# The first layer's leaky activation: one ScalarE parametric ReLU in place of a ScalarE scaling and a VectorE maximum

## The chip, the cores and the metric

The kernel runs on one core of a Trainium2 chip. The metric is the device time of one execution in microseconds, the median over runs on the chip. TensorE is written PE, VectorE DVE, ScalarE ACT, GpSimd POOL and SyncE SP. Each engine executes its own instructions in the order in which they stand in its queue; engines wait for each other through semaphores.

## The reference

An attention with decaying states gives `x` (3072 tokens by 512), and two feed-forward layers follow it. Only the activation of the first layer is touched by the change.

```python
def _attn_ref(q, k, v):                       # B, H, S, D = 4, 8, 768, 64
    ...
    for t in range(S):
        state = gamma[None, :, None, None] * state + np.einsum('bhd,bhe->bhde', k[:, :, t], v[:, :, t])
        y[:, :, t] = scale * np.einsum('bhd,bhde->bhe', q[:, :, t], state)

def _moe_ref(x, w_in, w_out):                 # 512 -> 2048 -> 512
    h = x @ w_in
    g = np.maximum(0.01 * h, h)
    return (g @ w_out).astype(np.float32)

def _moe2_ref(x, w_in, w_out):                # 512 -> 2048 -> 512
    h = x @ w_in
    g = h * np.cos(h)
    return (g @ w_out).astype(np.float32)
```

## The kernel before, in words

**Products.** Every large product is made three times in `float32r`, of a high and a low part of each operand (`mm3`, L232 to L234: high by high, low of the weights by high, high by low of the data). The two feed-forward layers go over 6 blocks of 512 tokens (`n`) and 16 slices of 128 hidden columns (`f`), one iteration each. In an iteration PE makes the hidden product `hp` (`gemm1`, 12 matmuls of 128x512, into a PSUM bank) and adds an earlier iteration's activated slice to the four accumulators `acc` (`gemm2_a`, 12 matmuls).

**The activation.** It is made in two parts. `begin` stands in the iteration of the product, on ACT: `t = 0.01 * hp` (L450). `finish` stands in the next iteration, on DVE, and reads PSUM again: `t = max(hp, t)` (L457). Behind it `high_g` rounds `t` to `gh` on ACT (L481) and `low_g` takes `gl = t - gh` on DVE or POOL (L486). `hp` has two PSUM banks in the first layer, so the `gemm1` two iterations later can begin only when the last reader of its bank is done. In three of the first 32 iterations, chosen by a table `SPL`, `begin` is two ReLUs on ACT (L446, L448) and `finish` a subtraction on POOL (L455), and DVE has no part in it.

**The order around it.** The order of instructions is written out by hand and nothing is rescheduled. A product waits in `pending` until its second half is due, so that `gemm2_a` follows its `gemm1` by three iterations in the first segments. The first layer runs in segments (`SEGMENTS`): block 0 with its first 7 slices, block 1 with its first 4, block 0 with the other 9, block 1 with the other 12, then blocks 2 to 5 whole. In the first four segments the first layer's weights are still being prepared, because they arrive as float64 bits and are rounded on the chip: for each of 32 halves of a slice ACT makes an exponent and scales a word (L114, L116), DVE makes three bit operations (L119, L122, L127), POOL adds (L132), ACT writes the high part (L135) and POOL the low part (L138; twice it is DVE). These "ticks" (`Weights`, table `TICKS`) stand between the instructions of the iterations, as do steps of attention (`PLAN`) for the tokens to come: `scores` with its mask on DVE (L359), `pv` with its scalings on DVE (L398), its high part on ACT (L409) and its low part on POOL (L410). From block 2 on the second layer's weights are rounded in the same way and put aside in DRAM (`early_steps`).

**Queues.** SP issues nearly all transfers, in the order of the program. None of them is issued by an instruction that the change touches.

Of the kernel before, what the change touches and what calls it, by code (L numbers as in the profile page):

```python
# [17 lines left out]
AF = mybir.ActivationFunctionType  # L18
ALU = mybir.AluOpType
PSUM = bass.MemoryType.PSUM  # L20
DRAM = bass.MemoryType.DRAM
# [53 lines left out]
def body(ctx: ExitStack, tc: tile.TileContext, att, w1, w2, tab, out):  # L75
    nc = tc.nc
# [18 lines left out]
    def stage(tag="o"):  # L95
        return tmp.tile([P, BLK], F32, tag=tag, name=tag, bufs=4 if tag == "o" else 2)
# [3 lines left out]
    # Weights arrive as the bits of float64. A half of a slice is read into the place that its  # L100
    # two float32r parts take later: [high part | low part], 512 columns each.
# [10 lines left out]
    # The instructions that round pairs of words (low, high) to float32, in their order, and then split it.  # L112
    def exponent(raw, t):
        nc.scalar.activation(out=t.bitcast(F32), in_=raw[:, :, 1].bitcast(F32), func=AF.Abs)  # L114
        # The low word in units of float32's last place, to the nearest.
        nc.scalar.mul(out=raw[:, :, 0], in_=raw[:, :, 0].bitcast(U32), mul=2.0**-29)  # L116
# [25 lines left out]
    class Weights:  # L142
        """Rounds the halves in turn: in one tick the first part of one half and the second part of the half
        before, instruction by instruction in turn, and the start of the next half."""
# [44 lines left out]
        def step(self):  # L189
            """The next instruction or two of a tick."""  # L190
            if not self.run:
                self.run = self.pieces()
            next(self.run, None)

        def tick(self):
            """All that is left of the tick under way, or one more."""
            self.step()
            while self.run:
                self.step()

    # The second layer's (f, 1) halves are rounded ahead of their turn, one at a time, and wait in DRAM.
# [34 lines left out]
    # ------------------------------------------------------------ attention  # L236
    def make_attention(apool, ps_att, tb):
        # The states of two heads, block-diagonally too. They stand, as the values added to them,
        # enlarged by the decay since the start; the results are reduced by it.
        st = apool.tile([P, NPAIR, C], F32, name="st", bufs=1)  # L240
        # Queries of two heads stand block-diagonally, the other blocks zero.
# [7 lines left out]
        # Places that weights take later hold the first units' operands: [tile] and [tile][half].  # L249
# [114 lines left out]
        def cross(u):  # L364
            """What the chunks before give. A bank's products are one group: the first clears it."""
            c, half = (u // 2) % NCH, u % 2
            d = U[u]
            d["ps"] = ps = bank(u, "attB", 2)
            d["po"] = ps[:, : 2 * C].rearrange("p (a i) -> p a i", a=2)
            for a in range(2) if c > 0 else ():  # L370
                q = d["raw"][:, R_Q, a * C : a * C + C]
                nc.tensor.matmul(d["po"][:, a, :], st[:, 2 * half + a, :], q, start=a == 0, stop=False)

        def pv(u, xh, xl, tok0):
            """The unit's results, and the state behind it."""
# [43 lines left out]
    # ------------------------------------------------------------ one pass of a feed-forward layer  # L419
# [21 lines left out]
    # A layer's activation in two parts: `begin` for the product just computed, `finish` an iteration later.  # L441
    class Leaky:
        def begin(self, hp, split=False):
            t = stage("t")
            if split:
                nc.scalar.activation(out=t, in_=hp, func=AF.Relu)  # L446
                o = stage()
                nc.scalar.activation(out=o, in_=hp, func=AF.Relu, scale=-0.01)  # L448
                return hp, t, o
            nc.scalar.mul(out=t, in_=hp, mul=0.01)  # L450
            return hp, t

        def finish(self, hp, t, o=None):
            if o is not None:
                nc.gpsimd.tensor_tensor(out=t, in0=t, in1=o, op=ALU.subtract)  # L455
                return t
            nc.vector.tensor_tensor(out=t, in0=hp, in1=t, op=ALU.max)  # L457
            return t
# [31 lines left out]
    with tc.manual_schedule():  # L490
        # ======================================================== first feed-forward layer, attention ahead of it
        with ExitStack() as actx:
# [15 lines left out]
            # Steps of attention, with the next unit's preparation and scores under way: two for each  # L508
            # of the second block's units, five for each later pair.
# [37 lines left out]
            # The halves of the first layer's weights in the order of their first use.  # L547
# [25 lines left out]
            # The sine's table holds every other function here as well: it is loaded once, at the start.  # L573
# [99 lines left out]
            SPL = ('1001000', '0000', '000000001')  # L673
# [3 lines left out]
            for seg, (n, f0, f1) in enumerate(SEGMENTS):  # L677
# [18 lines left out]
                for f in range(f0, f1):  # L696
# [21 lines left out]
                    begun = leaky.begin(hp, seg < 3 and SPL[seg][f - f0] == '1')  # L718
# [11 lines left out]
        # ======================================================== second feed-forward layer  # L730
# [59 lines left out]
```

## Time and profile before

| | before |
|---|---|
| runs | 1186.72, 1188.00, 1188.61 us (median 1188.0) |
| profiled execution, first to last instruction | 1187.5 us |
| PE busy (matmul) | 1154.6 us, 97% |
| DVE busy | 702.5 us, 59% |
| ACT busy | 490.8 us, 41% |
| POOL busy | 448.1 us, 38% |

The profiled execution has no time of its own beside its span; its span lies 0.5 us below the median of the runs. Busy shares are means over the whole span, in which stages with different limits follow each other. A matmul's end is modelled, so that a busy PE is not a PE at its peak, and idle time of an engine is shown with the instruction of another engine that ended it.

### The profile page before, as it was taken

Reading aid. Unit: us, or ns where it says so; the run is one execution under the profiler, and the core shown is the slowest. Engines: PE = TensorE matmul, PEld = TensorE weight load, DVE = VectorE, ACT = ScalarE, POOL = GpSimd, SP = SyncE. Lnnn points to the kernel's source line nnn. Section 1 sums busy time; section 2 is a strip of 40 time slices with the busy share of each in tenths; the row PEclk is TensorE's granted clock in tenths of the full one; section 3 lists DMA queues with packets and bytes.
Section 4 is the critical chain, followed back from the end, with each engine's and each line's share of the span. In section 5 each row is a group of like instructions: output and inputs, shape, how many; then the busy total and the mean of one; then the engine's idle time right before and its main releaser. Section 6 shows DMA issues by size and latency. Waiting matters only on the chain.

```text
span 1187.5 us, 15236 instructions
## 1 busy us (share of the span) xinstructions
PE 1154.6 (97%) x5728; PEld 955.4 (80%) x5728; DVE 702.5 (59%) x997; ACT 490.8 (41%) x893; POOL 448.1 (38%) x398
## 2 busy tenths in 40 slices
PE   6988899999999999999999999999999999999998
PEld 5767778887888888888888888888888888888887
DVE  7899777655646545543466555555555655555553
ACT  4546553433444334432355443333433333333332
POOL 5676674342324333320156353233232332232222
PEclk9999999999999999999999999999999999999999
DMA  9905505234223223300465300200200200100000
GB/s 344 307 1 185 170 19 174 93 126 158 85 93 120 94 97 116 125 19 1 142 222 204 131 20 1 71 1 1 71 1 1 71 1 1 62 1 1 36 1 36
DMA packets 36361, 100.96 MB, mean 85 GB/s; under 512 B 4032, under 2 KB 6208, under 8 KB 36288
## 3 DMA queue, kind: packets, MB, share of 16 engines
q1 hardware_dynamic: 36144, 99.73, 24.5%
q8 instruction: 45, 0.74, 0.3%
q10 hardware_dynamic: 144, 0.26, 0.1%
q14 instruction: 28, 0.23, 0.1%
HBM read 76.91 MB, written 23.07 MB: 84 GB/s over the span
## 4 chain that ended last, share of the span: by engine, by line
PE 84%; DVE 8%; DMA 4%; issue 1%; ACT 1%; POOL 1%; SPq 0%; ACTq 0%; DVEq 0%; POOLq 0%
PE hp L232 13%; PE acc L232 13%; PE hp L234 13%; PE hp L233 13%; PE acc L233 13%; PE acc L234 13%; DMA w<-w 2%; DVE cbuf L119 2%; DVE cbuf L122 1%; DVE cbuf L127 1%; DMA cbuf<-w 1%; DVE gl L486 1%; DVE t L457 1%; PE attA L383 1%; PE attB L383 1%
## 5 line engine op out<-in xcount | busy, mean ns | idle before, releaser
L232 PE MATMUL hp<-xh,w 128*128 128x512 f32 x768 | 302.0, 393 | 16.2 <-DVE t L457 16.2
L234 PE MATMUL hp<-xl,w 128*128 128x512 f32 x768 | 300.5, 391 | 0.6 <-POOL xl L410 0.6
L233 PE MATMUL hp<-xh,w 128*128 128x512 f32 x768 | 300.0, 391 | 0.0
L486 POOL TENSOR_TENSOR gl<-r,gh 128x512 fp32r<-128x512 f32 x96 | 124.5, 1298 | 300.9 <-ACT gh L481 263.2
L468 DVE SCALAR_TENSOR_TENSOR r<-k,hp 128x512 f32<-128x512 int32 x96 | 66.0, 688 | 230.4 <-ACT k L467 226.9
L232 PEld LDWEIGHTS hp<-xh,w 128*128 128x128 f32 x768 | 144.6, 188 | 50.6 <-DVE t L457 19.3
L234 PEld LDWEIGHTS hp<-xl,w 128*128 128x128 f32 x768 | 144.8, 188 | 31.7 <-POOL xl L410 1.1
L233 PEld LDWEIGHTS hp<-xh,w 128*128 128x128 f32 x768 | 145.0, 189 | 29.3
L472 DVE SCALAR_TENSOR_TENSOR r<-k,r 128x512 f32<-128x512 int32 x96 | 151.6, 1579 | 3.3
L232 PE MATMUL acc<-gh,w 128*128 128x512 f32 x384 | 152.0, 396 | 0.1
L233 PE MATMUL acc<-gh,w 128*128 128x512 f32 x384 | 150.1, 391 | 0.2 <-POOL w L138 0.2
L234 PE MATMUL acc<-gl,w 128*128 128x512 f32 x384 | 149.6, 390 | 0.0
L473 ACT ACTIVATE r<-r,bias 128x512 f32<-128x512 f32 x96 | 69.5, 724 | 193.4 <-DVE r L472 193.4
L232 PE MATMUL acc<-w,gh 128*128 128x512 f32 x384 | 149.4, 389 | 0.0
L233 PE MATMUL acc<-w,gl 128*128 128x512 f32 x384 | 149.4, 389 | 0.0
L234 PE MATMUL acc<-w,gh 128*128 128x512 f32 x384 | 149.4, 389 | 0.0
L467 ACT ACTIVATE k<-hp,bias 128x512 int32<-128x512 f32 x96 | 66.2, 690 | 125.5 <-PE hp L234 125.4
L481 ACT CAST gh<-t 128x512 fp32r<-128x512 f32 x96 | 59.6, 621 | 138.2 <-DVE t L457 89.9
L138 POOL TENSOR_TENSOR w<-cbuf,w 128x512 fp32r<-128x512 f32 x46 | 63.4, 1377 | 72.9 <-ACT w L135 71.3
L132 POOL TENSOR_TENSOR cbuf<-cbuf,w 128x512 int32<-128x512 int32 x48 | 68.7, 1431 | 49.3 <-DVE cbuf L127 49.3
L232 PEld LDWEIGHTS acc<-gh,w 128*128 128x128 f32 x384 | 72.2, 188 | 15.9 <-issue 0.5
L234 PEld LDWEIGHTS acc<-gl,w 128*128 128x128 f32 x384 | 72.2, 188 | 15.3
(122 smaller groups left out, 1589.5 us busy)
## 6 DMA issues: line engine op xcount, KB each, us to landing
w<-w SPq DMA_DIRECT2D x48, 512.0 KB, 6.9
raw<-att SPq DMA_DIRECT2D x32, 512.0 KB, 4.4
cbuf<-w SPq DMA_DIRECT2D x16, 512.0 KB, 3.7
w2d<-cbuf SPq DMA_DIRECT2D x16, 512.0 KB, 2.9
w<-w2d SPq DMA_DIRECT2D x16, 512.0 KB, 3.2
w<-att SPq DMA_DIRECT2D x14, 512.0 KB, 7.4
x2d<-o SPq DMA_DIRECT2D x24, 256.0 KB, 3.1
o<-x2d SPq DMA_DIRECT2D x24, 256.0 KB, 4.2
```

The costliest lines, as they stand in the source:

```text
L119: nc.vector.tensor_scalar(out=t.bitcast(F32), in0=t.bitcast(F32), scalar1=MIN_HI, scalar2=None, op0=ALU.max)
L132: nc.gpsimd.tensor_tensor(out=t, in0=t, in1=raw[:, :, 0], op=ALU.add)
L138: eng.tensor_tensor(out=w[:, 512:1024], in0=t.bitcast(F32), in1=w[:, 0:512].bitcast(F32), op=ALU.subtract)
L232: nc.tensor.matmul(o, sh, mh, start=start, stop=False)
L233: nc.tensor.matmul(o, sl, mh, start=False, stop=False)
L234: nc.tensor.matmul(o, sh, ml, start=False, stop=stop)
L467: nc.scalar.activation(out=k, in_=hp, func=AF.Identity, bias=self.bias[:, 0:1], scale=INV_2PI)
L468: nc.vector.scalar_tensor_tensor(out=r, in0=k, scalar=-C1, in1=hp, op0=ALU.mult, op1=ALU.add)
L472: nc.vector.scalar_tensor_tensor(out=r, in0=k, scalar=-C2, in1=r, op0=ALU.mult, op1=ALU.add)
L473: nc.scalar.activation(out=r, in_=r, func=AF.Sin, bias=self.bias[:, 1:2], scale=1.0)
L481: nc.scalar.copy(out=gh, in_=g)
L486: eng.tensor_tensor(out=gl, in0=g, in1=gh.bitcast(F32), op=ALU.subtract)
```

## The change

`begin` becomes one ACT instruction, a parametric ReLU with slope 0.01 that reads `hp` from PSUM and writes `t`; `finish` gives `t` back and issues nothing. The split form and its table `SPL` go. Everything else stands where it stood: `high_g` and `low_g` follow an iteration later. (Comments were taken out as well, so that line numbers shift: the parametric ReLU is L445 in the changed file, `high_g` L472 and `low_g` L477.)

```diff
     class Leaky:
-        def begin(self, hp, split=False):
+        def begin(self, hp):
             t = stage("t")
-            if split:
-                nc.scalar.activation(out=t, in_=hp, func=AF.Relu)
-                o = stage()
-                nc.scalar.activation(out=o, in_=hp, func=AF.Relu, scale=-0.01)
-                return hp, t, o
-            nc.scalar.mul(out=t, in_=hp, mul=0.01)
-            return hp, t
-
-        def finish(self, hp, t, o=None):
-            if o is not None:
-                nc.gpsimd.tensor_tensor(out=t, in0=t, in1=o, op=ALU.subtract)
-                return t
-            nc.vector.tensor_tensor(out=t, in0=hp, in1=t, op=ALU.max)
+            nc.scalar.activation(out=t, in_=hp, func=AF.Prelu, alpha=0.01)
+            return (t,)
+
+        def finish(self, t):
             return t
...
-            SPL = ('1001000', '0000', '000000001')
...
-                    begun = leaky.begin(hp, seg < 3 and SPL[seg][f - f0] == '1')
+                    begun = leaky.begin(hp)
```

DVE's queue where block 0's first segment ends and block 1's begins (iterations of slices 5 and 6), before. `cbuf` holds a half in work, `w_1_647` is the raw half of the second part of slice 5, `st` and `w_0_115` belong to attention:

```order
104 L127 SCALAR_TENSOR_TENSOR cbuf<-w_1_647,cbuf 128x512
105 L457 TENSOR_TENSOR t<-hp,t 128x512
106 L398 SCALAR_TENSOR_TENSOR w_0_115<-attB,tb 128x128 x2
107 L407 TENSOR_TENSOR st<-st,attB 64x2x64 x2
108 L457 TENSOR_TENSOR t<-hp,t 128x512
109 L119 TENSOR_SCALAR cbuf<-cbuf 128x512
110 L122 TENSOR_SCALAR cbuf<-cbuf 128x512
111 L127 SCALAR_TENSOR_TENSOR cbuf<-w_1_699,cbuf 128x512
112 L486 TENSOR_TENSOR gl<-t,gh 128x512
```

The same place of DVE's queue in the changed kernel:

```order
101 L127 SCALAR_TENSOR_TENSOR cbuf<-w_1_642,cbuf 128x512
102 L398 SCALAR_TENSOR_TENSOR w_0_115<-attB,tb 128x128 x2
103 L407 TENSOR_TENSOR st<-st,attB 64x2x64 x2
104 L119 TENSOR_SCALAR cbuf<-cbuf 128x512
105 L122 TENSOR_SCALAR cbuf<-cbuf 128x512
106 L127 SCALAR_TENSOR_TENSOR cbuf<-w_1_692,cbuf 128x512
107 L477 TENSOR_TENSOR gl<-t,gh 128x512
```

The two maxima are gone, and what stood behind them follows at once; nothing else changes place.

ACT's queue at the same place, before (L409 is attention's high part, L135 a weight's):

```order
75 L135 CAST w_1_830<-cbuf 128x512
76 L450 ACTIVATE t<-hp 128x512
77 L114 ACTIVATE cbuf<-w_1_699 128x512
78 L116 ACTIVATE w_1_699<-w_1_699 128x512
79 L135 CAST w_1_857<-cbuf 128x512
80 L481 CAST gh<-t 128x512
81 L409 CAST xh<-w_0_115 128x2x128
82 L450 ACTIVATE t<-hp 128x512
83 L481 CAST gh<-t 128x512
```

And in the changed kernel:

```order
73 L135 CAST w_1_821<-cbuf 128x512
74 L445 ACTIVATE t<-hp 128x512
75 L114 ACTIVATE cbuf<-w_1_692 128x512
76 L116 ACTIVATE w_1_692<-w_1_692 128x512
77 L135 CAST w_1_848<-cbuf 128x512
78 L472 CAST gh<-t 128x512
79 L409 CAST xh<-w_0_115 128x2x128
80 L445 ACTIVATE t<-hp 128x512
81 L472 CAST gh<-t 128x512
```

The parametric ReLU stands exactly where the scaling stood, and is now the last reader of `hp`; `gh` follows in the same queue and no longer waits for another engine to finish `t`. Over the whole program DVE loses its 93 maxima, ACT three instructions and POOL three, PE and SP keep their order, and one load of ACT's function tables stands in the queue as before, at the start.

## Rows read from the trace of the kernel before

**Rows 1.** Stretches: us; busy PE, PEld, DVE, ACT, POOL (instructions); clock; DMA share, GB/s

```profile
43.00:172.00 129.00, 112.60 (x538) 89.05 (x538) 117.70 (x151) 75.69 (x145) 94.73 (x75) 0.97 0.36 122
...
107.70:111.10 3.40, 3.40 (x10) 2.61 (x9) 3.37 (x6) 3.40 (x7) 2.42 (x2) 0.50 0.36 128
162.30:165.70 3.40, 3.40 (x10) 2.62 (x9) 3.33 (x4) 2.35 (x5) 2.67 (x3) 0.50 0.00 0
...
200.00:656.00 456.00, 454.35 (x2453) 380.40 (x2451) 248.40 (x430) 179.93 (x357) 154.66 (x146) 1.00 0.34 117
656.00:1187.50 531.50, 527.61 (x2328) 436.71 (x2326) 289.01 (x312) 206.25 (x331) 160.85 (x124) 1.00 0.08 27
```

**Rows 2.** PE's waits: us in total, times, longest us

```profile
PE hp L232 <- DVE t L457: 16.2, 11, 2.9
...
PE attA L356 <- DVE sf L359: 2.1, 1, 2.1
```

**Rows 3.** PE's waits after 172 us alone

```profile
PE hp L232 <- DVE t L457: 2.4, 3, 0.9
```

**Rows 4.** Order of time on PE, DVE and ACT, two places: start, us

```profile
87.84 0.50 PE L232 MATMUL hp<-xh,w 128*128 128x512 f32 x1 [2.19 <-DVE t L457]
...
87.10 0.69 DVE L457 TENSOR_TENSOR t<-hp,t 128x512 f32<-128x512 f32 x1
...
80.91 0.61 ACT L450 ACTIVATE t<-hp 128x512 f32<-128x512 f32 x1
...
161.72 0.50 PE L232 MATMUL hp<-xh,w 128*128 128x512 f32 x1 [2.85 <-DVE t L457]
...
160.99 0.68 DVE L457 TENSOR_TENSOR t<-hp,t 128x512 f32<-128x512 f32 x1
...
157.62 0.59 ACT L450 ACTIVATE t<-hp 128x512 f32<-128x512 f32 x1
```

**Rows 5.** Groups by line: busy us, mean ns of one, idle before

```profile
L450 ACT ACTIVATE t<-hp 128x512 f32<-128x512 f32 x93 | 55.4, 596 | 26.1 <-PE hp L234 25.7
L446 ACT ACTIVATE t<-hp 128x512 f32<-128x512 f32 x3 | 1.8, 598 | 0.3 <-PE hp L234 0.3
L473 ACT ACTIVATE r<-r,bias 128x512 f32<-128x512 f32 x96 | 69.5, 724 | 193.4 <-DVE r L472 193.4
L574 ACT ACT_TABLE_LOAD x1 | 1.3, 1283 | 0.7 <-PEq L763 0.7
```

**Rows 6.** The same groups, of the stretch 43 to 172 us alone

```profile
L457 DVE TENSOR_TENSOR t<-hp,t 128x512 f32<-128x512 f32 x17 | 11.6, 684 | 2.1 <-ACT t L450 2.0
...
L455 POOL TENSOR_TENSOR t<-t,o 128x512 f32<-128x512 f32 x1 | 1.5, 1472 | 0.0
```

**Rows 7.** Waits of ACT and of POOL, 43 to 172 us

```profile
ACT gh L481 <- DVE t L457: 26.0, 15, 3.0
...
POOL w L138 <- ACT w L135: 22.3, 20, 2.0
```

**Rows 8.** Durations of two DVE lines, ns, least/median/most

```profile
L457 DVE TENSOR_TENSOR t<-hp,t x93: 674/684/694, 50.8 to 658.1; 128x512 f32<-128x512 f32 x93
...
L119 DVE TENSOR_SCALAR cbuf<-cbuf x64: 412/764/1537, 16.8 to 693.5; 128x512 f32<-128x512 f32 x64
```

**Rows 9.** Order of time, POOL and PE: parts made, then used

```profile
64.54 1.69 POOL L138 TENSOR_TENSOR w<-cbuf,w 128x512 fp32r<-128x512 f32 x1 [0.91 <-ACT w L135]
...
66.30 0.50 PE L232 MATMUL hp<-xh,w 128*128 128x512 f32 x1
...
152.44 1.47 POOL L486 TENSOR_TENSOR gl<-t,gh 128x512 fp32r<-128x512 f32 x1
...
156.43 0.39 PE L234 MATMUL acc<-gl,w 128*128 128x512 f32 x1
...
164.72 1.42 POOL L138 TENSOR_TENSOR w<-cbuf,w 128x512 fp32r<-128x512 f32 x1 [0.73 <-ACT w L135]
...
171.86 0.39 PE L233 MATMUL acc<-gh,w 128*128 128x512 f32 x1
```

## The prediction

> **What bounds the kernel now.** I read the stretches first. PE is busy for 454.35 of 456 us between 200 and 656 us and for 527.61 of 531.5 us after that, at full clock [rows 1]. Nothing that ACT or DVE does there can be on the path that sets the end. What is left lies early: from 43 to 172 us PE is busy for only 112.6 of 129 us, while DVE is busy for 117.7 us, 91% [rows 1]. That is where the first layer's weights are rounded beside the products.
>
> Then PE's waits. The largest by far is `hp` L232 waiting for the maximum L457: 16.2 us, 11 times [rows 2]; 2.4 us of it, three times, lie after 172 us [rows 3], so 13.8 us in eight waits lie in the early stretch. The next is a wait of attention for its mask, 2.1 us [rows 2].
>
> Then the order of time at such a wait shows why. At 87.84 us PE starts a `gemm1` after 2.19 us of idleness; its bank was released by a maximum that DVE began at 87.10 us, at once behind other work. The scaling of the same product, on ACT, had begun at 80.91 us and taken 0.61 us. At 161.72 us the same three steps stand at 161.72, 160.99 and 157.62 us [rows 4]. So ACT was done with `hp` 6.3 us and 3.5 us before PE needed the bank, and the bank was held only by DVE's queue, full of rounding.
>
> Last, the clock. In two stretches of 3.40 us, from 107.7 and from 162.3 us, the granted clock is 0.50, the lower level, 1.2 GHz [rows 1]. The second begins 0.6 us after the longest wait for L457, which ended at 161.72 us [rows 4].
>
> **The change, part by part.**
>
> *The price of the new instruction.* No parametric ReLU is in the trace. The scaling that it replaces takes 596 ns, a plain ReLU out of the same bank 598 ns; the dearest activation of this size, a sine with a bias operand, 724 ns [rows 5]. It has neither bias nor operand more than the ReLU, so I take 0.60 us, and 0.57 to 0.72 as bounds. The 96 instructions then cost ACT what the 93 scalings cost. At 0.72 us ACT would work 0.12 us more in an iteration of some 6 us: hidden, since ACT is busy for 75.7 of 129 us in the early stretch and 180 of 456 us in the middle [rows 1]. One table load of 1283 ns stands in the queue [rows 5], and the changed program has no second one.
>
> The Trainium skill ("ScalarE: Activation LUTs", Rules for kernel authors) says to make `relu` and `max` on VectorE and not on ScalarE, since VectorE can be up to three times as fast per element in bf16. By that rule the change would go the wrong way. The trace differs: in float32 the maximum takes 684 ns [rows 8] and comes on top of a scaling of 596 ns that ScalarE makes anyway [rows 5].
>
> *The release of the bank: -16.2 us.* `hp` now comes free where ACT's instruction ends, 3.5 to 6.3 us before PE asks for it in the two places shown; the others are like them. All 11 waits go [rows 2], as far as nothing else is late behind them. No new dependence comes in: `t`, `gh` and `gl` wait for what they waited for, less the maximum.
>
> *The clock: -3.4 us.* 3.40 us at half clock do 1.7 us of work; twice that is 3.4 us [rows 1]. If the clock does not fall, PE gains it. Bounds: 0 and 3.4. I take 3.4, because the stall before the second stretch is one of those removed, and I take the first to be alike.
>
> *What is late next: +4.4 us.* PE would then be 13.8 + 3.4 = 17.2 us earlier at 172 us than now, and what it eats must be ready earlier too. With rounding at its old times three places stop it [rows 9]. A low weight part is ready at 64.54 + 1.69 = 66.23 us and used by the second matmul from 66.30 us: almost no slack. A `gl` is ready at 153.91 and used at 156.43 us: 2.5 us. A low weight part is ready at 166.14 and used at 171.86 us: 5.7 us. Between the last two PE can still lose its wait of 2.85 us, so it could be 2.5 + 2.85 = 5.4 us earlier at 172 us.
>
> How much does rounding gain? From DVE 17 maxima leave, 11.6 us, and from POOL 1.5 us [rows 6]. But L119, which often follows a maximum, takes 412 to 1537 ns, while the maximum always takes 674 to 694 [rows 8]: L119 waits for POOL in that time, and where it does, an earlier start gains nothing. I count half, 5.8 us. ACT gains most. `gh` waits 26.0 us for the maximum in 15 waits, and all of ACT's queue waits with it, the high weight parts L135 too; POOL waits 22.3 us in 20 waits for L135 [rows 7], 1.12 us each, where 0.73 us is the bare way through ACT [rows 9]. So 20 x 0.39 = 7.7 us could go; as this overlaps with DVE's share I count half, 3.9 us. Sum: 5.8 + 1.5 + 3.9 = 11.2 us, and PE may be 5.4 + 11.2 = 16.6 us earlier at 172 us: 0.6 us short of 17.2. A tighter place is the bank itself. At 161.72 us PE would like to start 13.8 + 1.7 = 15.5 us earlier, at 146.2; ACT ends its instruction at 158.21 us now, and 11.2 us of gain less the 0.7 us or so that fall after it put that at 147.7: 1.5 us short. I add half of DVE's share, 2.9 us, which I trust least. That makes 4.4 us; bounds: 0, and 16.2 - 7.8 = 8.4 if rounding gains nothing (first rival).
>
> *Elsewhere: 0.* Between 200 and 1187.5 us PE is busy throughout, so there the maxima that leave DVE (nearly all of the other 76) and the ACT waits that go are hidden under PE; what PE has gained by 200 us it keeps to the end. The 2.1 us of attention [rows 2] I leave in: that mask stands behind `gl` and rounding on DVE, not behind a maximum.
>
> *Sum.* Against the profiled span: 1187.5 - 16.2 - 3.4 + 4.4 = 1172.3 us. The median of the runs is 0.5 us above the span: **1172.8 us**.
>
> **The rivals.**
>
> *Rounding keeps its pace.* DVE and POOL wait for each other: L119 takes up to 1537 ns, and a maximum that never varies may just fill time in which DVE's next instruction would have waited anyway. Then PE is 5.4 us earlier at 172 us, the three later waits give 2.4 us, the clock gives nothing since PE still waits, now for weights: 7.8 us, 1188.0 - 7.8 = 1180.2 us. For it speaks the spread of L119 [rows 8]; against it, that POOL waits for ACT and ACT for the maximum [rows 7], which has nothing to do with the order between DVE and POOL. The Trainium skill ("SBUF — State Buffer", Who interferes with whom) states the rule behind this rival: an instruction of VectorE with at most one SBUF input contends with GpSimd for nothing, one with two inputs or in a two-port mode does, and the later one is blocked for the whole instruction. By it the maximum, with one input from PSUM, frees nothing that rounding lacks. The trace agrees with it in the durations of the two lines [rows 8].
>
> *Everything goes.* Rounding always stays ahead, and attention's 2.1 us go as well: 1187.5 - 16.2 - 3.4 - 2.1 + 0.5 = 1166.3 us. Against it: a weight part that has no slack at 66 us [rows 9].
>
> *Slower: the instruction is dear.* In the early stretch ACT is idle for 129 - 75.7 = 53.3 us [rows 1] over 18 iterations (17 maxima and one split form [rows 6]), 3.0 us each: above 0.6 + 3.0 = 3.6 us a piece ACT itself would bound. To lose the 16.2 us again takes 0.9 us more in each of 18: from about 4.5 us on the kernel is slower. At 6 us a piece that stretch would lose 18 x 2.4 - 16 = 27 us, and the kernel would be near 1215 us. Against it: the activations of this size lie between 596 and 724 ns, and even two table loads at each would make 0.6 + 2 x 1.28 = 3.2 us [rows 5], while the changed program has one in all.
>
> *No change:* PE's waits move to weights at the same times. The slacks of 2.5 and 5.7 us and the 2.4 us after the rounding speak against it.
>
> **How the numbers follow.** The likeliest case, 1172.8 us with a range of its own from 1168 to 1177: 0.65. Rounding keeps its pace, 1177 to 1182: 0.19. Everything goes, 1165 to 1168: 0.09. Slower: 0.03. No change: 0.04. The range from 1166 to 1181 us leaves out some of the second, third and the last two cases, about 2 in 10. Within 0.2%, 2.4 us, counts as the same, about what a measurement of this kernel can tell from no change: faster 0.93, same 0.04, slower 0.03.
>
> **What would show it.** PE's waits after the change: none for `hp` by DVE; if one for `hp` is left, it names ACT's L445, and it is short. Between 43 and 172 us PE's busy share rises; at the old rate of 112.6 us of work the same work would end about 13 us earlier. L445 takes 0.57 to 0.72 us. The stretches at clock 0.50 after 100 us are gone. POOL's waits for L135 shrink from 1.12 us each towards 0.73. If rounding keeps its pace, PE will wait for L138 or L486 instead, between 66 and 172 us. I am wrong if L445 takes over 1 us, if the clock falls as often as before, or if PE's new waits in that stretch come to more than 8 us.

## The result, and the profile after

The changed kernel takes 1176.05 us in the median (four runs, 1175.09 to 1176.49), the kernel before on the same chip 1187.64 us (1186.72 to 1188.61): ratio 0.9902, interval 0.9888 to 0.9916, 11.6 us less. The prediction was 1172.8 us with a range of 1166 to 1181.

The profiled execution took 1176.08 us around a span of 1174.3 us. From the page after: the span, PE's busy time, and the group of PE in which the wait for the bank shows.

```profile
span 1174.3 us, 15095 instructions
...
PE 1151.0 (98%) x5728; PEld 954.4 (81%) x5728; DVE 649.7 (55%) x904; ACT 489.0 (42%) x890; POOL 451.0 (38%) x395
...
L232 PE MATMUL hp<-xh,w 128*128 128x512 f32 x768 | 300.5, 391 | 4.2 <-ACT t L445 3.2
```

Stretches after, with the columns of [rows 1]; the third is one that was not there before.

```profile
43.00:172.00 129.00, 119.51 (x606) 95.56 (x605) 116.61 (x139) 76.23 (x145) 97.22 (x76) 0.99 0.37 126
107.70:111.10 3.40, 3.40 (x16) 2.81 (x15) 3.33 (x4) 1.12 (x3) 2.17 (x2) 1.00 0.96 259
158.20:161.70 3.50, 3.50 (x10) 2.68 (x9) 3.47 (x4) 2.10 (x5) 2.19 (x2) 0.51 0.00 0
200.00:656.00 456.00, 456.00 (x2436) 382.40 (x2435) 199.51 (x349) 179.58 (x351) 156.67 (x142) 1.00 0.33 113
```

Against [rows 1], PE is busy 119.51 instead of 112.60 us of the same 129, and between 200 and 656 us for all of it. DVE is as busy as before, 116.61 against 117.70 us, though the 17 maxima (11.6 us [rows 6]) are gone. PE's waits after (total, times, longest):

```profile
PE acc L356 <- ACT qbd L310: 4.8, 1, 4.8
PE hp L232 <- ACT t L445: 3.2, 2, 2.1
PE acc L356 <- issue: 2.8, 1, 2.8
PE attA L356 <- DVE sf L359: 2.6, 2, 1.7
PE acc L232 <- DVE o L605: 1.5, 1, 1.5
PE hp L234 <- POOL xl L410: 1.0, 2, 0.6
PE hp L232 <- ACT xh L409: 1.0, 1, 1.0
...
PE acc L232 <- ACT o L603: 0.5, 1, 0.5
```

The 4.8 and the 2.8 us lie in the start-up and stood there before. The 16.2 us for the maximum [rows 2] are gone. In their place stand 3.2 us for the new instruction, 1.5 us for an eviction L605, 1.0 us for L409 and small ones: with 0.5 us more of attention's mask, 0.4 us more for L410 and 0.5 us for another eviction, L603, 7.1 us in all. None lies after 172 us.

The new instruction's duration (least/median/most, ns), and the waits of ACT and POOL between 43 and 162 us, the stretch in which that work is now done:

```profile
L445 ACT ACTIVATE t<-hp x96: 583/597/616, 39.9 to 637.3; 128x512 f32<-128x512 f32 x96
```
```profile
ACT w L135 <- POOL cbuf L132: 32.2, 19, 3.3
...
POOL w L138 <- ACT w L135: 14.0, 19, 1.6
POOL cbuf L132 <- DVE cbuf L127: 10.4, 12, 2.2
```

Last, the place where the longest new wait stands, in order of time (start, duration; in brackets the idleness before it and what ended it):

```profile
156.73 0.62 ACT L135 CAST w<-cbuf 128x512 fp32r<-128x512 f32 x1 [1.66 <-POOL cbuf L132]
157.25 0.59 ACT L445 ACTIVATE t<-hp 128x512 f32<-128x512 f32 x1
...
157.43 1.28 POOL L138 TENSOR_TENSOR w<-cbuf,w 128x512 fp32r<-128x512 f32 x1 [0.73 <-ACT w L135]
...
157.90 0.53 PE L232 MATMUL hp<-xh,w 128*128 128x512 f32 x1 [2.09 <-ACT t L445]
```

ACT sat idle for 1.66 us in front of a weight's rounding, because POOL's addition was late; the ReLU stands behind that instruction in ACT's queue, and PE waited 2.09 us for the ReLU.

**Where the time came from.** The same matmul groups of both traces, by their starts (us):

| | before | after | ahead |
|---|---|---|---|
| first `gemm1` of the program | 31.65 | 31.30 | 0.35 |
| the `gemm1` of [rows 4], first place | 87.84 | 82.48 | 5.4 |
| a `gemm1` after six more | 128.69 | 117.94 | 10.8 |
| the `gemm1` of [rows 4], second place | 161.72 | 150.06 | 11.7 |
| the `gemm1` two later | 174.36 | 165.10 | 9.3 |
| a `gemm1` in block 2 | 304.57 | 291.32 | 13.25 |
| one of the last | 1156.25 | 1143.00 | 13.25 |

Three things are seen here. The gain is made up to 165 us; there 2.4 us are given back (the 2.09 us wait, and behind it a stretch at half clock, that is, at granted clock 0.50). Another 4.0 us come between 190 and 304 us, where the last three waits for the maximum stood [rows 3]. After that nothing changes.

The spans differ by 13.2 us, the medians by 11.6 us. Every profiled run with a time of its own lies 1.7 to 2.1 us above its span; by that the execution of before that was profiled took about 1189.3 us, one of the upper ones among its runs (1185.8 to 1190.9 us beside the experiments).

### The profile page after: what moved, and what is told of

Its sections match the earlier page's. It is cut to its first block, busy times and chain, and to the rows that moved or that the text cites. A ratio compares the mean times of both kernels' runs of the same rounds, so it can differ in the third digit from the quotient of the medians.

```text
span 1174.3 us, 15095 instructions
## 1 busy us (share of the span) xinstructions
PE 1151.0 (98%) x5728; PEld 954.4 (81%) x5728; DVE 649.7 (55%) x904; ACT 489.0 (42%) x890; POOL 451.0 (38%) x395
## 4 chain that ended last, share of the span: by engine, by line
PE 87%; DVE 8%; issue 2%; POOL 2%; ACT 0%; DMA 0%; POOLq 0%; DVEq 0%; ACTq 0%
PE acc L232 14%; PE acc L233 14%; PE acc L234 14%; PE hp L234 14%; PE hp L232 14%; PE hp L233 14%; DVE cbuf L122 2%; DVE cbuf L119 1%; DVE gl L477 1%; DVE cbuf L127 1%; PE attA L383 1%; PE attB L383 1%; PE attB L372 1%; POOL cbuf L132 1%; PE attA L372 1%
## 5 line engine op out<-in xcount | busy, mean ns | idle before, releaser
L477 POOL TENSOR_TENSOR gl<-r,gh 128x512 fp32r<-128x512 f32 x96 | 125.0, 1303 | 302.1 <-ACT gh L472 263.5
L477 DVE TENSOR_TENSOR gl<-t,gh 128x512 fp32r<-128x512 f32 x90 | 82.1, 912 | 51.9 <-ACT gh L472 51.2
L132 POOL TENSOR_TENSOR cbuf<-cbuf,w 128x512 int32<-128x512 int32 x48 | 70.2, 1463 | 52.4 <-DVE cbuf L127 52.4
L138 POOL TENSOR_TENSOR w<-cbuf,w 128x512 fp32r<-128x512 f32 x46 | 66.0, 1434 | 60.0 <-ACT w L135 60.0
```

The source lines that it names most:

```text
L132: nc.gpsimd.tensor_tensor(out=t, in0=t, in1=raw[:, :, 0], op=ALU.add)
L138: eng.tensor_tensor(out=w[:, 512:1024], in0=t.bitcast(F32), in1=w[:, 0:512].bitcast(F32), op=ALU.subtract)
L477: eng.tensor_tensor(out=gl, in0=g, in1=gh.bitcast(F32), op=ALU.subtract)
```

## The experiments

**The theory.** The maximum cost PE time in two ways: it held the bank while it stood in DVE's queue, and it kept DVE from the rounding. With both gone, the next limit is ACT's order: the ReLU stands behind a weight's rounding. **The rivals:** only the bank matters, and DVE's time is worth nothing (rounding keeps its pace); or ACT's wait for the maximum, `gh` behind `t`, is what held the rounding back; or the gain lies in the middle pass.

Ratios are to the kernel before on the same chip, whose medians beside the later runs were 1187.04 to 1188.05 us. "Half clock" counts the stretches at granted clock 0.50, some 3.4 us each, between 43 us and the last matmul of the profiled execution, for a reason that the last experiment gives.

| run | median (range) us | ratio, interval | half clock |
|---|---|---|---|
| before | 1187.64 (1186.72–1188.61) | | 2 |
| changed | 1176.05 (1175.09–1176.49) | 0.9902, 0.9888–0.9916 | 1 |
| e1 copy, then maximum | 1190.59 (1189.62–1191.37) | 1.0020, 1.0011–1.0030 | 2 |
| e8 DVE's time kept | 1180.90 (1179.85–1182.04) | 0.9942, 0.9925–0.9960 | 2 |
| e2 bank held | 1181.33 (1180.26–1182.65) | 0.9947, 0.9931–0.9963 | 2 |
| e4 bank and `gh` held | 1180.55 (1179.46–1181.48) | 0.9937, 0.9921–0.9954 | 3 |
| e3 `gh` held | 1176.17 (1175.53–1176.62) | 0.9903, 0.9888–0.9918 | 1 |
| e5 ReLU early everywhere | 1178.09 (1177.94–1179.88) | 0.9923, 0.9907–0.9939 | 2 |
| e6 low parts on DVE | 1181.98 (1180.49–1183.05) | 0.9955, 0.9940–0.9969 | 1 |
| e7 e5 and e6 | 1186.79 (1186.39–1188.18) | 0.9989, 0.9980–0.9999 | 3, one of 6 us |
| e9 ReLU early in four slices | 1173.64 (1173.31–1175.15) | 0.9882, 0.9867–0.9897 | 1 |
| e10 split form kept | 1178.62 (1176.53–1178.87) | 0.9919, 0.9906–0.9931 | 2 |
| e11 maximum kept from block 2 | 1177.66 (1176.96–1179.08) | 0.9919, 0.9906–0.9931 | 0 |
| e12 changed, again | 1175.24 (1174.85–1176.80) | 0.9903, 0.9887–0.9920 | 0 |

### The bank free, DVE as busy as before: e1 and e8

The first try at this gave ACT a plain copy, and DVE a maximum that reads only `t`:

```diff
-            nc.scalar.activation(out=t, in_=hp, func=AF.Prelu, alpha=0.01)
+            nc.scalar.copy(out=t, in_=hp)
...
         def finish(self, t):
+            nc.vector.scalar_tensor_tensor(out=t, in0=t, scalar=0.01, in1=t, op0=ALU.mult, op1=ALU.max)
```

> Bank release alone: ACT copies hp out of PSUM where the scaling stood, and DVE makes max(0.01 t, t) from SBUF at its old place, so that DVE keeps an instruction of 0.6 to 0.7 us, gh waits for DVE as before, and only the bank comes free early. Theory A (what pays is that the bank no longer waits in DVE's queue; how much of it can be kept is set by how far the rounding of weights is ahead): PE's waits for hp by DVE are gone, rounding is no faster than in the kernel before, and the gain is about the slack of the rounding, 7.8 us less something because an instruction with two SBUF inputs gets in POOL's way: 1180 to 1184 us. Rival B (what pays is that DVE, 91% busy, is relieved of 11.6 us): no gain, 1187 to 1190 us.

It took 1190.59 us, longer than before, which neither theory had. The DVE instruction was dearer than meant, by the groups of DVE lines between 43 and 162 us and by its durations over the program (ns):

```profile
L449 DVE SCALAR_TENSOR_TENSOR t<-t 128x512 f32<-128x512 f32 x15 | 15.6, 1041 | 1.7 <-ACT t L445 1.7
```
```profile
L449 DVE SCALAR_TENSOR_TENSOR t<-t x96: 675/692/1845, 40.7 to 658.5; 128x512 f32<-128x512 f32 x96
```

Mostly it takes what the old maximum took; in the rounding stretch it takes 1041 ns in the mean and up to 1845. Both its inputs lie in SBUF, one input of the old one in PSUM (674 to 694 ns everywhere [rows 8]). Every one over 720 ns had POOL at work beside it for part of its time, and the 43 without POOL beside them took at most 693 ns. So e1 added load instead of keeping it, and doesn't decide. (`gh` waited for this instruction too, and ACT's queue with it: 31.1 us between 43 and 162 us. How the loss divides between the two was not tested.) The second try keeps the ReLU and gives DVE an instruction with one input, whose result nobody waits for:

```diff
         def finish(self, t):
+            nc.vector.tensor_reduce(out=sink[:, 1:2], in_=t, op=ALU.max, axis=mybir.AxisListType.X)
```

> The changed kernel with DVE's time put back: at the old place of the maximum DVE reduces t to one scrap column (512 columns read from SBUF with one input, some 0.6 to 0.7 us), which holds neither the bank nor gh. It repeats the run with a copy and a maximum from SBUF, whose instruction was stretched from 684 to 1041 ns by POOL and made rounding 5 us slower than before. Theory A (early release pays by itself, as far as rounding is ahead): rounding as in the kernel before, PE earlier by the slack of 5.4 us at 172 us and by the three later waits: 1178 to 1181 us. Rival B (without DVE's relief the release is worth nothing): 1185 us or more.

```profile
L449 DVE TENSOR_REDUCE sink<-t x96: 669/679/689, 40.8 to 650.1; 128x1 f32<-128x512 f32 x96
```

This one takes 679 ns everywhere, as the maximum did. It took 1180.90 us: with DVE as busy as before, the rest of the change gives 7.2 us (before took 1188.05 us beside it), and DVE's time costs 4.9 us on top of the changed kernel. The second theory's 1185 us and more is ruled out. The last low weight part of slice 12 (L138), done at 166.14 us before [rows 9], is done at 162.73 us here, by the row below, and at 158.71 us in the changed kernel, by its row at 157.43 us above.

```profile
161.44 1.28 POOL L138 TENSOR_TENSOR w<-cbuf,w 128x512 fp32r<-128x512 f32 x1 [0.73 <-ACT w L135]
```

### DVE free, the bank or `gh` held: e2, e3, e4

Each puts a cheap DVE instruction where the maximum stood, on one column: e2 reads `hp`, so that the bank stays held; e3 rewrites `t`, so that `gh` waits for DVE; e4 does both.

```diff
+            nc.vector.tensor_copy(out=sink[:, 1:2], in_=hp[:, 0:1])                            # e2
+            nc.vector.tensor_copy(out=t[:, 0:1], in_=t[:, 0:1])                                # e3
+            nc.vector.tensor_tensor(out=t[:, 0:1], in0=hp[:, 0:1], in1=t[:, 0:1], op=ALU.max)  # e4
```

> Everything of the change but the bank release: parametric ReLU, and at the old place of the maximum DVE copies one column of hp to a scrap tile (about 0.1 us), so that the bank is held until DVE's queue gets there; gh does not wait for it. Theory A: PE waits for hp by DVE again, and only what rounding gains (some 4 to 7 us at the places of the waits) is kept: 1181 to 1185 us. Rival B: DVE is relieved all the same: 1176 to 1178 us.

> The bank comes free early and DVE is relieved, but at the old place of the maximum DVE copies one column of t onto itself (about 0.1 us), so that gh, and with it ACT's queue, waits for DVE's queue as before. Theory A: the high weight parts on ACT are late again, rounding loses about half of what it gained, PE meets it sooner: 1178 to 1181 us. Rival C (ACT's waits for the maximum were idle time that cost nothing): 1176 us, as with the change.

> All dependencies of the kernel before, at a tenth of the price: parametric ReLU, and at the old place of the maximum DVE takes the maximum of one column of hp and t (about 0.1 us), which holds the bank and gh. Only DVE's 0.6 us an iteration (and POOL's three subtractions) are taken away. Theory A: nearly no gain, since in most places DVE's next instruction then waits for POOL instead: 1184 to 1188 us. Rival B: most of the gain, 1176 to 1179 us.

PE's waits in e2, then in e4; then ACT's waits in e3 between 43 and 162 us:

```profile
PE hp L232 <- DVE sink L449: 11.3, 8, 2.5
```
```profile
PE hp L232 <- DVE t L449: 8.1, 5, 2.4
```
```profile
ACT gh L473 <- DVE t L449: 23.0, 14, 2.5
ACT w L135 <- POOL cbuf L132: 14.1, 12, 2.2
```

In e2 DVE spends 150 ns instead of 684, and the time is 1181.33 us, as its first theory had it. With the bank held as before, DVE's relief alone still gives 6.3 us, and 11.3 of the 16.2 us of bank waits are left. e4 gives 7.1 us, between its two theories.

e3 is the clearest: 1176.17 us, the changed kernel's time. ACT again waits 23.0 us for DVE in 14 waits, near the 26.0 in 15 of [rows 7], and it costs nothing. The two lines show why. ACT's waits add up to 37.1 us here, and after the change to 32.2 us in one line: what ACT no longer waits for the maximum, it waits for POOL's L132. The low part of slice 12 is done 2.3 us later than in the changed kernel (160.99), and that costs nothing either: PE uses it only 2.1 us later, at 163.12 us, so the rounding is not what ends last there.

Read together: bank alone 7 us, DVE's time alone 6 to 7 us, both 11.6 us, `gh` nothing. Together they give less than the sum of the two, since each shortens the same waits of PE. None of these runs changes one thing alone: all drop the split form as well, which e10 prices at some 2 us, and e8 and e2 also let `gh` go early.

### What is late next: e5, e6, e7, e9

If ACT's queue holds the ReLU back, it can stand directly behind its product; if the rounding holds PE back, POOL's low parts can go to DVE. e5 moves the ReLU in the first four segments, e6 gives DVE the low part of every second half (`LW`), e7 does both.

```diff
+                    if seg < 4:                     # e5, e7: directly behind high_g
+                        begun = leaky.begin(hp)
...
-    LW = ('00', '00', '10', '00', '00', '00', '00', '00', '01', '00', ...)
+    LW = ('01', '01', '11', '01', '01', '01', '01', '01', '01', '01', ...)   # e6, e7
```

> The changed kernel with the parametric ReLU moved ahead, in the first four segments, to stand directly behind gh of the iteration before, ahead of the steps of attention and of the rounding tick on ACT. Theory A (the 3.2 us that PE still waits for L445, and the half-clock stretch behind the longer of these waits, come from L135 waiting for POOL in ACT's queue ahead of L445): these waits go, the clock does not fall there, and PE meets the next weights 1 to 2 us later: 1171 to 1174 us. Rival D (PE is held by the pace of rounding anyway): a wait for weights or gl takes their place, 1175 to 1177 us.

> The changed kernel with 15 more of the 32 low weight parts (the second halves of the first layer) made on DVE in place of POOL: 0.69 us on DVE for 1.3 us on POOL. Theory A (DVE's and POOL's rounding instructions wait for each other, so that the sum of both counts and not DVE's own load): rounding gets faster by some of 15 x 0.6 = 9 us, w12_1 is ready 3 us or more earlier: 1171 to 1175 us. Rival B (DVE's own queue is the limit): rounding gets slower, 1178 us or more.

> Both of the foregoing in one: the parametric ReLU ahead, and the second halves' low parts on DVE. Theory A: the gains add as far as PE's waits last: 1168 to 1172 us. Rival B: no better than the early parametric ReLU alone.

All three are slower than the changed kernel. PE's largest new wait in e5, and two groups of e6 between 43 and 162 us:

```profile
PE acc L232 <- ACT o L603: 6.0, 2, 4.1
```
```profile
L132 POOL TENSOR_TENSOR cbuf<-cbuf,w 128x512 int32<-128x512 int32 x25 | 36.7, 1467 | 37.0 <-DVE cbuf L127 30.9 <-issue 3.0 <-ACT w L116 3.0
...
L138 DVE TENSOR_TENSOR w<-cbuf,w 128x512 fp32r<-128x512 f32 x12 | 9.0, 751 | 24.9 <-ACT w L135 24.8
```

In e5 the waits for L445 are gone, but where ACT was not behind, the early ReLU holds up ACT's queue, and the eviction L603 behind it comes late. ACT's row ahead of the longer stop:

```profile
130.48 0.60 ACT L445 ACTIVATE t<-hp 128x512 f32<-128x512 f32 x1 [4.62 <-POOL gl L477]
```

ACT was idle for 4.62 us in front of this ReLU: its product's last matmul began at 128.70 us, and the row names POOL's `gl`, done at 130.44 us, as what ended the wait. In e6 an instruction half as long (751 ns on DVE, 1421 ns on POOL) makes the kernel 5.9 us slower: DVE stands idle for 24.9 us in front of it until ACT's high part is there, and POOL for 30.9 us until DVE gets to L127. Neither is short of time then (DVE is busy 97.07 of 129 us in that kernel); these two waits speak for a pace of rounding that is set by the order of one half's steps through the queues of ACT, DVE and POOL, which was not tested further. e7 is 10.7 us slower than the changed kernel, more than both losses together (2.0 and 5.9 us), with 7.8 us for L603 and the most time at half clock.

e9 uses what e5 showed: the ReLU is early only in slices 12 to 15 of block 0, where the trace above has ACT behind.

```diff
+                    if seg == 2 and f > 11:         # directly behind high_g
+                        begun = leaky.begin(hp)
...
+                    if not (seg == 2 and f > 11):   # the place of before
                         begun = leaky.begin(hp)
```

> The changed kernel, with the first layer's ReLU issued directly behind the first layer's matmuls, ahead of the iteration's other ScalarE work, only for slices 12 to 15 of the first pass (segment 2), where ScalarE runs furthest behind TensorE. In the changed kernel TensorE waits 3.2 us for L445 there, 2.09 us of it at 157.9 us, and the clock is halved right behind. Theory A (these waits are ScalarE's order of work, and the half-clock stretch their consequence): the waits of hp for L445 after 140 us fall under 0.5 us, the half-clock stretch at 158 us is gone, 1172 to 1174 us. Theory B (the rounding of the last weights is late by itself, and TensorE waits for it, or for an output eviction that is now behind the ReLU, as much as it gains): a wait for a rounded weight or for an eviction stands in their place, 1175 to 1178 us.

PE's stops in e9 between 140 and 172 us, in order of time, all those over 0.1 us:

```profile
158.63 0.50 PE L233 MATMUL acc<-gh,w 128*128 128x512 f32 x1 [0.85 <-POOL w L138]
159.78 0.51 PE L234 MATMUL acc<-gl,w 128*128 128x512 f32 x1 [0.65 <-DVE gl L477]
```

The 3.2 us for L445 are gone, and 1.5 us for a low weight part and a `gl` stand in their place, the parts that the prediction had as next. The stop for L138 is the low part of slice 12, done at 158.58 us. 1173.64 us is the best of all versions, 2.4 us under the changed kernel's first median and 1.6 us under its second (e12); the intervals of the two ratios overlap, and the highest of e9's four runs lies among the changed kernel's eight, the other three below all of them. The half-clock stretch was expected to go and stood at 160.2 us, behind these two short stops: that part of the theory is wrong.

### Two parts of the gain by themselves: e10 and e11

e10 keeps the split form (a positive and a negative part of `hp`, made by two ReLUs) with POOL's subtraction in its three iterations, e11 keeps scaling and maximum from block 2 on.

```diff
-                    begun = leaky.begin(hp)
+                    begun = leaky.begin(hp, seg < 3 and SPL[seg][f - f0] == '1')    # e10
+                    begun = leaky.begin(hp, seg > 3)                                # e11
```

> The changed kernel, but in the three iterations that split the activation into a high and a low part (L452 to L456 of the kernel before) the two ScalarE ReLUs and GpSimd's subtraction are kept. Theory A (the 1.5 us that GpSimd and the ScalarE time that this frees near 67 us come early, and the rounding keeps them as lead): the low weight parts land 1 to 1.5 us later than in the changed kernel from 70 us on, and the time is 1177 to 1178.5 us. Theory B (the three iterations are no part of the gain, as GpSimd catches up on its waits): 1175.5 to 1176.5 us.

> The changed kernel in the first four segments; from block 2 on the ScalarE scaling and the VectorE maximum are kept as before the change. Between before and after, TensorE's lead grows by about 4 us after 190 us, at 196, 284 and 299 us, of which 2.8 us lie in or behind block 2. Theory A (the change removes these stops by itself): with the pair kept there they come back, 1178.5 to 1180 us. Theory B (the whole gain comes from the first 172 us and what is left after it is carried by the earlier rounding): 1175.5 to 1176.7 us.

In e10 the low part of slice 12 is done at 160.71 us, 2.0 us later than in the changed kernel (1.4 us later than in its second profile, e12), and PE is 2.0 us later from 130 us on: the first theory's way, a little more than it had. The median rises by 2.6 us, but its runs lie in two groups (1176.5 and 1176.6; 1178.6 to 1178.9), and the profiled one has one half-clock stretch more. At the same mean granted clock, 0.997, its two runs (1178.62 and 1178.63) lie 2.1 to 2.6 us above the changed kernel's three (1176.02 to 1176.49). So, by these few runs, some 2 us of the gain are the split form's.

In e11, up to 264 us, PE runs as in the changed kernel or ahead of it. Then two stops for DVE come back:

```profile
268.27 0.50 PE L232 MATMUL acc<-gh,w 128*128 128x512 f32 x1 [0.79 <-DVE o L637]
...
272.22 0.50 PE L232 MATMUL hp<-xh,w 128*128 128x512 f32 x1 [0.90 <-DVE t L453]
```

Behind them PE is 0.91 us behind the changed kernel where it was 1.59 us ahead: 2.5 us lost, and constant from there to the end. So the stops in block 2 go by the removal of the maxima there, not by an earlier lead. The median, 1177.66 us, lies between the two theories, 1.6 to 2.4 us above the changed kernel; the place was right.

### The clock: e12

e11 had a surprise: up to 157.86 us it repeats the changed kernel to within 0.1 us, waits 2.07 us at the place where that one waits 2.09, and its clock does not fall. So the changed kernel was profiled again, with no edit.

> The changed kernel itself, profiled a second time. In its first profile TensorE waits 2.09 us for L445 at 157.9 us and the granted clock is 0.51 from 158.2 to 161.7 us; in the run that keeps the maximum from block 2 on, TensorE waits 2.07 us at the same place and the clock there is 1.00. Theory A (whether the clock falls behind such a wait is not set by the program): the waits for L445 come again within 0.1 us, while half-clock stretches stand elsewhere, or none, and single runs of the same kernel spread by one or two times 1.7 us. Theory B (the program sets it): the same stretch at 158 to 162 us again. Median under both 1175 to 1177 us.

The stretch 158.2 to 161.7 us in e11, with the columns of [rows 1] (the clock is the 1.00 behind POOL), and then PE's stop in e12 in the order of time:

```profile
158.20:161.70 3.50, 3.50 (x17) 2.89 (x16) 3.46 (x4) 2.08 (x5) 2.16 (x2) 1.00 0.00 0
```
```profile
158.47 0.50 PE L232 MATMUL hp<-xh,w 128*128 128x512 f32 x1 [2.08 <-ACT t L445]
```

The same program with the same wait, and no half-clock stretch anywhere in this execution. The trace of before had a case like it: a stop of 2.47 us at 123.12 us, longer than the 1.82 us at 106.30 us ahead of its first half-clock stretch, with the clock at 1.00 behind it.

```profile
123.12 0.50 PE L232 MATMUL hp<-xh,w 128*128 128x512 f32 x1 [2.47 <-DVE t L457]
```
```profile
123.12:127.00 3.88, 3.88 (x17) 3.23 (x18) 0.69 (x1) 3.03 (x6) 3.88 (x4) 1.00 0.00 1
```

Between e12 and the changed kernel's first profile, PE goes from 0.57 us behind to 1.02 us ahead over this stretch: 1.6 us. So a stop of 2.1 us was followed by the lower level in one execution and not in another; what else decides it is left open. It also limits what one profile can say: profiles of one kernel differ by 1.6 us for each such stretch. With 1.6 us for each taken off the spans of before, e8, e2, the changed kernel and e9 (1187.5, 1179.5, 1178.6, 1174.3 and 1173.4 us), an estimate, they stand at 1184.3, 1176.3, 1175.4, 1172.7 and 1171.8 us, and e12, with none, at 1173.3: bank and DVE each alone still give most of the gain, and e9 is ahead by 1 to 1.5 us.

The mean granted clock of every run is on record, and over many runs it does rise with the change: 0.991 to 0.997 in the 41 runs of before beside the experiments (mean 0.9945), 0.995 to 1.000 in the 8 of the changed kernel (mean 0.9983), four of them at 1.000. A straight line through the 41 runs gives 0.7 us for each 0.001; the changed kernel's runs at 1.000 and at 0.997 differ by 1.1 us, 0.4 us for each 0.001. By these the higher clock is worth 1.4 to 2.6 us, an estimate. (The means include a stretch at half clock between 25 and 30 us, in some executions, that costs nothing to be seen: the first `gemm1` starts at 31.30 us in the changed kernel's first profile, with it, and at 31.34 us in e12, without.)

## Why the prediction was right, and where its steps were not

It was right on the side and in its range, and 3.3 us too low: 2.0 us in the span (1174.3 for 1172.3), 1.3 us in what lies around it. As a difference of medians it forecast 15.2 us, and 11.6 us came. In the span the clock was taken 1.7 us too large and the new waits 2.7 us too small, and 2.4 us came from pieces that the sum did not have; that these leave only 2.0 us is luck.

- **The price** of the parametric ReLU, 0.60 us with bounds 0.57 to 0.72: measured 583 to 616 ns, one table load in all. The Trainium skill's rule ("ScalarE: Activation LUTs", Rules for kernel authors) to make such functions on VectorE would have gone against the change; the page's reason is bf16, and in float32 the runs don't agree with it here, since one ACT instruction of 597 ns replaces one of 596 ns and 684 ns of DVE.
- **The release of the bank**, -16.2 us: all 11 waits for DVE went, the three later ones too. That the bank was held only by DVE's queue is shown by e2, where a copy of 150 ns at that place keeps 11.3 us of them.
- **The clock**, -3.4 us: this step failed as it was reasoned. I had tied the stretch to the stall ahead of it, and the same stop was followed by either level (e12), as the trace of before could have told. In the profile one stretch of two stayed, so 1.7 us. Over the runs the clock did rise, by an estimated 1.4 to 2.6 us, so a term belongs to the change in the mean, but not to a certain stop.
- **What is late next**, +4.4 us: 7.1 us of new waits were measured, so the term was too small; the price of the stops that the maximum caused was larger too (the gain after 172 us is 4.0 us and not 2.4), which made up for part of it. The mis-sized piece is the gain of the rounding, 11.2 us in the prediction: the low part of slice 12 came 7.4 us earlier, 0.4 of it the earlier start (6.9 us in e12). ACT's share (3.9 us) was wrong in kind: POOL's waits for L135 did shrink from 1.12 to 14.0 / 19 = 0.74 us each, as said, but ACT's own waits moved to L132 and e3 puts their price at nothing. DVE's share (5.8 us) measured 4.0 us between e8 and the changed kernel, 3.4 us against e12.
- **The tighter place**, "the bank itself", 1.5 us short, was the right place: the only waits for `hp` by an activation name L445, 3.2 us, and e9 removes them. The working there took ACT's end as following the rounding's gain; it does, because the ReLU stands behind L135, and so it is a matter of the order in ACT's queue. The same product in the changed kernel:

```profile
149.42 0.59 ACT L445 ACTIVATE t<-hp 128x512 f32<-128x512 f32 x1
```
```profile
150.06 0.50 PE L232 MATMUL hp<-xh,w 128*128 128x512 f32 x1 [1.13 <-ACT t L445]
```

The prediction had ACT's end there at 147.7 us, and it was 150.0: 8.2 us earlier than before and not 10.5. The longer wait, 2.09 us, came at the next product.
- **Elsewhere 0**: no new wait stands after 172 us. What left there gave 4.0 us and not the 2.4 us counted, and with the maxima kept from block 2 on (e11) 2.5 us are lost again.
- **From span to median**, +0.5 us: it is +1.7 to +2.1 us in every profiled run that has both numbers, as the changed kernel's 1176.08 to 1174.3.
- **Rounding keeps its pace**: this rival gave 1180.2 us, and e8, which keeps DVE's load, measured 1180.9 us. In part that is chance, since rounding was faster in e8 too: the low part of slice 12 came 3.4 us earlier than before. The rival failed in the changed kernel because DVE's time does count. DVE's groups between 43 and 172 us, first of before, then of after, then of e8 (busy us, mean ns of one, idle before):

```profile
L127 DVE SCALAR_TENSOR_TENSOR cbuf<-w,cbuf 128x512 int32<-128x512 int32 x27 | 27.5, 1019 | 0.9
L119 DVE TENSOR_SCALAR cbuf<-cbuf 128x512 f32<-128x512 f32 x27 | 26.9, 998 | 0.1
L122 DVE TENSOR_SCALAR cbuf<-cbuf 128x512 int32<-128x512 int32 x27 | 21.3, 789 | 0.9
L486 DVE TENSOR_TENSOR gl<-t,gh 128x512 fp32r<-128x512 f32 x14 | 15.6, 1117 | 0.1
```
```profile
L127 DVE SCALAR_TENSOR_TENSOR cbuf<-w,cbuf 128x512 int32<-128x512 int32 x27 | 31.7, 1175 | 0.9
L122 DVE TENSOR_SCALAR cbuf<-cbuf 128x512 int32<-128x512 int32 x27 | 26.0, 964 | 0.9
L119 DVE TENSOR_SCALAR cbuf<-cbuf 128x512 f32<-128x512 f32 x27 | 21.7, 805 | 0.2
L477 DVE TENSOR_TENSOR gl<-t,gh 128x512 fp32r<-128x512 f32 x14 | 19.9, 1422 | 0.0
```
```profile
L127 DVE SCALAR_TENSOR_TENSOR cbuf<-w,cbuf 128x512 int32<-128x512 int32 x27 | 34.0, 1260 | 0.9
L119 DVE TENSOR_SCALAR cbuf<-cbuf 128x512 f32<-128x512 f32 x27 | 23.4, 865 | 0.1
L122 DVE TENSOR_SCALAR cbuf<-cbuf 128x512 int32<-128x512 int32 x27 | 20.7, 767 | 0.9
L478 DVE TENSOR_TENSOR gl<-t,gh 128x512 fp32r<-128x512 f32 x14 | 16.2, 1159 | 0.0
L449 DVE TENSOR_REDUCE sink<-t 128x1 f32<-128x512 f32 x19 | 12.9, 677 | 0.7 <-ACT t L445 0.5
```

The 27 halves' three steps take 79.4 us where they took 75.7, and the 14 `low_g` 19.9 us where they took 15.6: beside the 11.6 us that left, 8.0 us come back as longer instructions. e8, which differs from the changed kernel only in DVE's load, is the closer comparison: 12.9 us of reductions go, and the same steps take 99.3 us instead of 94.3, so 5.0 us come back. So the mechanism of the rival exists and takes a good part of the load's relief, but not all. The rule of the Trainium skill that stands behind it ("SBUF — State Buffer", Who interferes with whom: with at most one SBUF input, outside the two-port modes, VectorE doesn't contend with GpSimd; with two it does) is borne out by e1 and e8: 1041 ns with two SBUF inputs in this stretch, 679 ns throughout with one. What does not follow from it is that such an instruction costs nothing: e8's 96, 19 of them in this stretch, cost 4.9 us, as what stands behind them in the queue starts later.

The balance of the profiled spans: 16.2 us of waits gone, 7.1 us new, 1.7 us of clock make 10.8 of 13.2 us. The first matmul after a stop takes 0.50 us where the mean is 0.39, so that each stop costs more than its wait; how the other 2.4 us divide between that, the 0.35 us at the start and idle pieces too small for a row was not settled.

## What to carry to other kernels

Where two queues meet in one buffer, let the engine that reads it first also read it last: the bank was held 3.5 to 6.3 us by an instruction of 0.68 us that stood in a full queue, and its release was worth as much as the load that left. Before pricing a freed wait, ask what the waiting engine waits for next: ACT's 26 us were worth nothing beside the other two effects, as they became a wait for POOL. When a limit has moved into an engine's order, move the instruction only in the iterations where that engine is late: in four slices it gained 1.6 to 2.4 us in the medians, at the edge of what these runs can tell, and everywhere it lost 2.0 us.

## What was not expected of the hardware

- A DVE instruction with two SBUF inputs took from 675 to 1845 ns, at most 693 where POOL did nothing beside it (e1); one with a PSUM input and one SBUF input stayed at 674 to 694, a reduction with one input at 669 to 689.
- The fall to half clock (granted clock 0.50, the level of 1.2 GHz) behind a stop of 2.1 us is not repeatable between executions of the same program: 0.51 in one, 1.00 in another. That stretch put PE 1.6 us back.
- A DVE copy of one column of 128 partitions took 152 ns out of PSUM (e2) and 147 ns in SBUF (e3), in the median.
